# Sliding-window attention and SwiGLU on one core: transposes of k and q for chunks 0 to 9 in 64x64 tiles, and another order of the opening

## The chip, the core and the metric

The kernel runs on one NeuronCore of a Trainium2 chip. Five engines have a queue each: TensorE (PE; its weight loads are shown apart as PEld), VectorE (DVE), ScalarE (ACT), GpSimd (POOL) and SyncE (SP). They take their instructions in the order written and wait for one another by semaphores. DMA transfers are issued from the queues of POOL, SP and ACT. Matrix products go from SBUF into PSUM, which has eight banks; VectorE and ScalarE read PSUM. The metric is the device time of one execution in microseconds; less is better.

## What is computed

Attention with a causal window of 64 over 8 batches, 8 heads, 576 positions and head dimension 64, and then a SwiGLU block over the 4608 tokens (512 to 1536 to 512):

```python
scores = scale * np.matmul(q, k.transpose(0, 1, 3, 2))
mask = (rel >= 0) & (rel < window)            # rel = query position - key position, window = 64
scores = np.where(mask, scores, -1000000000.0)
attn = np.exp(scores - np.max(scores, axis=-1, keepdims=True))
attn = attn / (np.sum(attn, axis=-1, keepdims=True) + 1e-09)
x = np.matmul(attn, v)                        # heads side by side: 4608 x 512
g = x @ w_gate
out = (g * (1.0 / (1.0 + np.exp(-g))) * (x @ w_val)) @ w_out
```

Inputs and output are float32.

## The kernel before

The 4608 tokens are 36 chunks of 128 for the attention and 9 column blocks of 512 for the FFN; work for both is interleaved by hand in `build`, and the order of the calls there is the order on every engine. `_Graph.op` records each operation with the tiles it reads and writes; `emit` turns the data dependences into semaphore waits, one place in the queue of one engine for each operation. All matrix products of one operation are one unit: they wait together and signal together.

For a chunk n the attention is: transpose k and q so that the head dimension lies on partitions (`kT`, `qT`); scores into two PSUM banks (`Sb` or `Sk`; in the opening `Sa` with `Sbias`, which puts the mask in by a matmul, and `So`); exp on ScalarE into `pt`; attention times v with a column of ones (`AVs`, `AVmm`, `AVpair`); reciprocal and product on VectorE into `xb` (`AVn`, lines 623 and 626); transpose to `xT` (`Xp` on TensorE with an eviction, or an SP DMA transpose). `F(c, fs)` is a gate and value product of 4 + 4 matmuls (line 888), tanh on ScalarE (869), two VectorE products (874, 876). `O(c, u)` is 12 matmuls with Wo (930), an eviction and a store.

The transposes of k and q come in three kinds:

- Chunks 0 to 3, and 6 and 7: `first_T` (lines 825 and 827). For chunks 0 and 1 the float32 input is loaded by SP and ACT into two halves and cast by `first_cast` (lines 260 for ScalarE and 261 for VectorE); eight 128x128 transposes of k go into one bank, eight of q into another. For the other chunks the cast happens in the GpSimd DMA, and sixteen transposes with 128 input rows and 64 output rows fill one bank for two chunks. `first_ev` copies one chunk from the bank.
- Chunks 4, 5, 8 and 9: `T2` (line 382), sixteen such transposes for k and sixteen for q, a bank each, and one copy of 1024 columns for both chunks.
- From chunk 10 on: `T`, an SP DMA transpose. These the change leaves alone.

`bank` takes the least recently touched bank that isn't held, `pair` an even and the following odd one. In the opening the mask matmuls and the scores of chunks 0 to 3, the transposes, `AVs` and `Xp` take their banks by this rule. Copies of v by half a chunk (`shift`) give `AVs` its keys of the chunk before; two of the six are on VectorE (chunk 1), four on GpSimd.

Of the kernel before, what the change touches and what calls it, by code (L numbers as in the profile page):

```python
# [153 lines left out]
class _Kernel:  # L154
# [216 lines left out]
    def T2(self, st, x):  # L371
        src = (self.ks2 if x == "k" else self.qs2)[st % 2]
        dst = self.kT if x == "k" else self.qT
        nz = self.NZ if x == "k" else self.ZQ
        bank, bk = self.bank("a")
        tb = bank.bitcast(BF).rearrange("p (c j t) -> p c j t", c=4, j=2)

        def pe(e):
            for c in range(4):
                for j in range(2):  # L380
                    for p in range(2):
                        r = e.transpose(tb[64 * p:64 * p + 64, c, j, :], src[:, 2 * c + p, j, :], self.ident[:, :])  # L382
            return r

        self.g.op("pe", pe, reads=["ident", ("s2", x, st % 2, 0), ("s2", x, st % 2, 1)], writes=[bk])
        a = tb.rearrange("p c j t -> p c t j")

        def ev(eng, lo=0, hi=2):
            z0 = (2 * st + lo) % nz
            if z0 + hi - lo > nz:  # L390
                ev(eng, 0, 1)
                ev(eng, 1, 2)
                return
            d = dst[:, :, 128 * z0:128 * (z0 + hi - lo)].rearrange("p c (t j) -> p c t j", j=2)
            self.copy(eng, d, a[:, :, 64 * lo:64 * hi, :], [bk], [(x + "T", z, b) for z in range(z0, z0 + hi - lo) for b in range(2)])

        return ev

# [5 lines left out]
    def Sa(self, n, bias=False):  # L404
        st = [n, self.pair(), False]
        if bias:
            self.Sbias(st)
        return st
# [149 lines left out]
    def AVa(self, n):  # L558
        bx = self.pair()
# [215 lines left out]
    def Xp(self, n, kind="a"):  # L775
        ix, it, u = n % 4, (n // 4) % self.NX, n % 4
        xb, xo = self.xb[ix], self.xT[it][:, :, 128 * u:128 * u + 128]
        bank, bk = self.bank(kind)
# [37 lines left out]
    def first_T(self, x, st=0):  # L816
        c, ckeys = self.first[x, 1] if st else (self.first[x][2], self.first[x][3] + self.first[x, 0])
        bank, bk = self.bank("a")
        tb = bank.bitcast(BF).rearrange("p (j t) -> p j t", j=8)

        def pe(e):
            for j in range(8):
                if st:
                    for p in range(2):
                        r = e.transpose(tb[64 * p:64 * p + 64, j, :], c[:, j, p, :], self.ident[:, :])  # L825
                else:
                    r = e.transpose(tb[:, j, :], c[:, j, :, :], self.ident[:, :])
            return r

        self.g.op("pe", pe, reads=["ident"] + ckeys, writes=[bk])  # L830
        return bank, bk

    def first_ev(self, x, n, eng, b, after=None):
        bank, bk = b
        dst = self.kT if x == "k" else self.qT
        g = 16 * (n % 2)
        a = bank.bitcast(BF).rearrange("p (j g c) -> p c g j", j=8, c=4)[:, :, g:g + 16, :]
        d = dst[:, :, 128 * n:128 * n + 128].rearrange("p c (g j) -> p c g j", j=8)
        return self.copy(eng, d, a, [bk], [(x + "T", n, 0), (x + "T", n, 1)], after)
# [180 lines left out]
    def build(self):  # L1020
        F, S, AV, X, T2, O = self.F, self.S, self.AV, self.X, self.T2, self.O
# [36 lines left out]
        a2 = self.AVa(2)  # L1058
# [3 lines left out]
        x1 = self.Xp(1)  # L1062
        x1("act")
        a3 = self.AVa(3)
        self.AVs(a3)
        x2 = self.Xp(2)
# [19 lines left out]
        T2(2, "k")("act")  # L1086
        T2(2, "q")("act")
# [152 lines left out]
```

## Time and profile before

| | |
|---|---|
| runs | 326.6, 326.89, 327.25 us; median 326.89 |
| profiled execution | span 324.8 us; no other time of it is given, and against the median 2.09 us lie around the span |
| busy share of the span | PE 98%, DVE 66%, ACT 39%, POOL 32% |
| first FFN matmul (line 888) | starts at 15.63 us |
| DMA | 39.83 MB, mean 123 GB/s |
| largest groups on PE | line 888 111.2 + 111.0 us, line 930 98.8 us |

Times in the profile are microseconds from the start of the span. A timeline row gives the start, the length, the engine, the line, the operation, what it writes and reads, and how many instructions were merged into it; in brackets stands the idle time before it and what ended that. A row of the chain of waits gives start, length and the work that the end of the program goes back to. A row of a stretch gives, for each engine, the busy microseconds and the number of instructions; after them come the granted clock, the DMA share and GB/s. TensorE's instructions are pipelined, so that the start of the next one comes well before the end that is shown.

### The profile page before, as it was taken

The numbers are of one execution on the slowest core, as the hardware profiler recorded it, in microseconds if no ns is written. First come the engines' busy times: TensorE is split into PE (matmuls) and PEld (weight loads), VectorE is DVE, ScalarE is ACT, GpSimd is POOL, SyncE is SP. The second block draws the span as 40 slices with busy tenths as digits, with TensorE's granted clock in tenths as the row PEclk, the third lists the DMA queues.
The fourth block names the chain that finished last, engine by engine and source line by source line (L and its number), as shares of the span: only waits on it lengthen the run. The fifth ranks groups of instructions, "written<-read, shape, count | busy, mean of one in ns | idle before, by whom it ended". The sixth has DMA issues, their size and how long they took to land.

```text
span 324.8 us, 7717 instructions
## 1 busy us (share of the span) xinstructions
PE 319.2 (98%) x3278; PEld 162.4 (50%) x3278; DVE 215.8 (66%) x400; ACT 125.8 (39%) x224; POOL 104.2 (32%) x134
## 2 busy tenths in 40 slices
PE   6999999999999999999999999999999999999996
PEld 5665565564544454545454444545454544444444
DVE  5886866688485966676768585958576767555510
ACT  3935563634332443333333242424242422222311
POOL 6999831142626061607060607060402000000000
DMA  7999999999999899959998998999687202000012
GB/s 189 179 191 186 205 172 167 161 150 149 158 138 167 128 100 137 163 109 152 119 115 122 146 141 81 146 132 163 71 110 96 69 32 67 32 34 32 32 67 97
DMA packets 154354, 39.83 MB, mean 123 GB/s; under 512 B 140368, under 2 KB 149328, under 8 KB 154320
## 3 DMA queue, kind: packets, MB, share of 16 engines
q0 software_dynamic: 104896, 18.36, 72.8%
q1 hardware_dynamic: 43952, 11.15, 24.7%
q10 hardware_dynamic: 5472, 9.83, 9.5%
q8 instruction: 26, 0.43, 0.5%
q14 instruction: 8, 0.07, 0.1%
HBM read 37.75 MB, written 9.44 MB: 145 GB/s over the span
## 4 chain that ended last, share of the span: by engine, by line
PE 96%; DMA 1%; ACT 1%; DVE 0%; SPq 0%; issue 0%
PE ps L888 58%; PE ps L930 29%; PE ps L692 2%; PE ps L514 2%; DMA hT<-in_q_dram 1%; PE ps L464 1%; PE ps L825 1%; ACT pt L447 1%; PE ps L382 1%; PE ps L420 1%; PE ps L582 1%; PE ps L468 0%; DVE ost L261 0%; PE ps L784 0%; PE ps L439 0%; ACT xT L260 0%
## 5 line engine op out<-in xcount | busy, mean ns | idle before, releaser
L874 DVE SCALAR_TENSOR_TENSOR uu<-sig,ps 128x512 bf16<-128x512 bf16 x108 | 73.9, 685 | 57.3 <-ACT sig L869 57.1
L888 PE MATMUL ps<-xT,Wg 128*128 128x512 bf16 (+1 forms) x456 | 111.2, 369 | 0.1
L888 PE MATMUL ps<-xT,Wv 128*128 128x512 bf16 (+1 forms) x456 | 111.0, 368 | 0.0
L869 ACT ACTIVATE sig<-ps 128x512 bf16<-128x512 f32 x108 | 65.1, 603 | 89.0 <-PE ps L888 89.0
L930 PE MATMUL ps<-Wo,hT 128*128 128x512 bf16 (+1 forms) x444 | 98.8, 374 | 0.0
L876 DVE SCALAR_TENSOR_TENSOR hT<-uu,ps 128x512 bf16<-128x512 bf16 x108 | 74.2, 687 | 3.7
L888 PEld LDWEIGHTS ps<-xT,Wv 128*128 128x128 bf16 x456 | 44.5, 98 | 48.4
L930 PEld LDWEIGHTS ps<-Wo,hT 128*128 128x128 bf16 x444 | 43.3, 98 | 49.2
L888 PEld LDWEIGHTS ps<-xT,Wg 128*128 128x128 bf16 x456 | 42.7, 98 | 45.5 <-ACT xT L260 0.6
L330 POOL DMA_DIRECT2D kn<-in_k_dram x29 | 24.9, 861 | 107.7 <-PE ps L888 103.7
L330 POOL DMA_DIRECT2D va<-in_v_dram x40 | 34.4, 889 | 34.0 <-PE ps L888 34.0
L260 ACT ACTIVATE ost<-ps 128x512 f32<-128x512 f32 (+1 forms) x22 | 12.9, 587 | 52.9 <-PE ps L930 52.9
L261 DVE COPY ost<-ps 128x512 f32<-128x512 f32 (+1 forms) x15 | 10.1, 674 | 30.1 <-PE ps L930 30.1
L524 ACT ACTIVATE pt<-ps 128x512 bf16<-128x512 f32 x36 | 18.6, 603 | 29.0 <-PE ps L514 29.0
L330 POOL DMA_DIRECT2D qn<-in_q_dram x29 | 25.1, 870 | 0.3 <-issue 0.3
L476 ACT ACTIVATE pt<-ps 128x512 bf16<-128x512 f32 x28 | 14.5, 603 | 12.9 <-PE ps L468 12.9
L727 DVE TENSOR_TENSOR xb<-ps,rc 128x512 bf16<-128x512 f32 (+2 forms) x39 | 18.8, 510 | 0.5
L692 PE MATMUL ps<-va,pt 64*64 64x65 bf16 x800 | 12.3, 192 | 0.0
L490 DVE TENSOR_TENSOR pt<-pt,kmask 128x1024 bf16<-128x1024 bf16 x18 | 11.5, 683 | 0.0
L692 PEld LDWEIGHTS ps<-va,pt 64*64 64x64 bf16 x800 | 10.3, 107 | 0.0
L723 DVE RECIPROCAL rc<-ps 128x8 f32<-128x8 f32 (+2 forms) x39 | 5.7, 174 | 6.5 <-PE ps L692 6.5
L490 DVE TENSOR_TENSOR pt<-pt,mask 128x1024 bf16<-128x1024 bf16 x14 | 9.3, 686 | 0.9 <-ACT pt L476 0.8
(76 smaller groups left out, 131.6 us busy)
## 6 DMA issues: line engine op xcount, KB each, us to landing
out_dram<-ost ACTq DMA_DIRECT2D x35, 256.0 KB, 2.9
va<-in_v_dram POOLq DMA_DIRECT2D x32, 128.0 KB, 5.5
kn<-in_k_dram POOLq DMA_DIRECT2D x23, 128.0 KB, 4.2
qn<-in_q_dram POOLq DMA_DIRECT2D x23, 128.0 KB, 4.5
Wg<-in_moe_w_gate_dram POOLq DMA_DIRECT2D x6, 256.0 KB, 6.6
Wv<-in_moe_w_val_dram POOLq DMA_DIRECT2D x6, 256.0 KB, 7.4
Wo<-in_moe_w_out_dram POOLq DMA_DIRECT2D x2, 768.0 KB, 15.3
ks<-in_k_dram POOLq DMA_DIRECT2D x2, 256.0 KB, 7.1
```

The source lines that it names most:

```text
L260: return self.g.op("act", lambda e: e.activation(d, a, ACTF.Copy), reads=reads, writes=writes, after=after)
L330: self.g.op("pool", lambda e, d=d, a=a: e.dma_start(d, a), writes=ks, dma=True, after=gate)
L476: g.op("act", lambda e, po=po, p=p: e.activation(po, sv[p], ACTF.Exp, scale=SCALE), reads=[bx[p][1]], writes=[pk[p]])
L490: self.g.op("dve", lambda e: e.tensor_tensor(pt, pt, m, ALU.mult), reads=pk + mk, writes=pk)
L524: g.op("act", lambda e, po=po, p=p: e.activation(po, sv[p], ACTF.Exp, scale=SCALE), reads=[bx[p][1]], writes=[pk[p]])
L692: x = e.matmul(o, ab[0], ab[1], start=first, stop=phase == 1, skip_group_check=True)
L727: g.op("dve", lambda e, av=av, hs=hs, w=w, rc=rc, xo=xo: e.tensor_tensor(xo[:, :, hs, :], av[:, :, :, 0:64], rc[:, :, hs].unsqueeze(3).to_ ...
L869: g.op("act", lambda e: e.activation(sig[:, 0:w], G[:, 0:w], ACTF.Tanh, scale=0.5), reads=[gk], writes=[("sig", i)])
L874: g.op("dve", lambda e: e.scalar_tensor_tensor(uu[:, 0:w], sig[:, 0:w], 1.0, G[:, 0:w], ALU.add, ALU.mult), reads=[("sig", i), gk], writes ...
L876: g.op("dve", lambda e: e.scalar_tensor_tensor(out, v3(uu), 0.5, v3(V), ALU.mult, ALU.mult), reads=[("uu", i), vk], writes=[("hT", ih, f) ...
L888: r = e.matmul(bank[:, a * n:a * n + n], W[:, kk, f * 128:f * 128 + 128], xT[:, kk, lo:hi], start=(kk == 0), stop=(kk == NK - 1))
L930: r = e.matmul(OB[:, 0:n], hT[:, f, 128 * u:128 * u + 128], self.Wo[:, f, lo:hi], start=(f == 0), stop=(f == NF - 1))
```

## The change

All transposes of chunks 0 to 9 on TensorE become 64x64: source rows 0 to 63 and 64 to 127 are transposed apart, with the matching quarter of the identity, and each row half goes to a bank of its own. With the order in which k and q are loaded, a row half is a chunk, so there is a bank per chunk. `T2` and the use of `first_T` for chunks 6 and 7 give way to `T64`, which does k and q of two chunks in one operation of 64 transposes (k in the first half of a bank, q in the second) and hands out four evictions of 512 columns; `Tkq2` puts all four on ScalarE. `first_T` for chunks 0 to 3 does 32 transposes into a pair of banks and hands out two evictions.

In the opening the pairs of banks are given by hand (`at`). ScalarE casts all of the second half of q, of which VectorE did five eighths; of the evictions of chunks 0 to 3, ScalarE has q0, k1 and q2 where it had q0, q2 and q3. The mask matmul of chunk 0 comes ahead of q's transposes, scores 0 and 1 come ahead of the second batch of transposes, `AVs(0)` ahead of scores 2 and 3, and VectorE's second shift behind the first `AVn`.

```diff
-    def pair(self):
+    def pair(self, at=None):
...
-        ok = [j for j in range(0, 8, 2) if not {j, j + 1} & self.held]
+        ok = [j for j in range(0, 8, 2) if not {j, j + 1} & self.held and at in (None, j)]
...
-    def T2(self, st, x):
...
+    def T64(self, st):
+        n = 2 * st
+        bx = self.two()
+        loads = []
+        for x in "kq":
+            if st == 3:
+                loads.append((x, *self.first[x, 1]))
+            else:
+                loads.append((x, (self.ks2 if x == "k" else self.qs2)[st % 2], [("s2", x, st % 2, i) for i in range(2)]))
...
+            for i, (x, src, _) in enumerate(loads):
+                for a in range(8):
+                    for u in range(2):
+                        r = slice(64 * u, 64 * u + 64)
+                        for p in range(2):
+                            o = bx[u][0].bitcast(BF)[64 * p:64 * p + 64, 512 * i + 64 * a:512 * i + 64 * a + 64]
+                            y = src[r, a, p, :] if st == 3 else src[r, 2 * (a // 2) + p, a % 2, :]
+                            z = e.transpose(o, y, self.ident[r, r])
+            return z
+
+        rd = ["ident"] + [k for _, _, ks in loads for k in ks]
+        self.g.op("pe", pe, reads=rd, writes=[b[1] for b in bx])
+
+        def ev(x, u, eng):
+            bank, bk = bx[u]
+            i = "kq".index(x)
+            a = bank.bitcast(BF)[:, 512 * i:512 * i + 512]
...
+            self.copy(eng, d, a, [bk], [(x + "T", z, 0), (x + "T", z, 1)])
+            left.discard((x, u))
+            if not any(v == u for _, v in left):
+                self.held.discard(bk[1])
+
+        left = {(x, u) for x in "kq" for u in range(2)}
         return ev
+
+    def Tkq2(self, st):
+        ev = self.T64(st)
+        for u in range(2):
+            for x in "kq":
+                ev(x, u, "act")
...
-    def first_T(self, x, st=0):
+    def first_T(self, x, st, at):
...
-        bank, bk = self.bank("a")
...
+        bx = self.pair(at)
...
-                if st:
+                for u in range(2):
+                    r = slice(64 * u, 64 * u + 64)
                     for p in range(2):
-                        r = e.transpose(tb[64 * p:64 * p + 64, j, :], c[:, j, p, :], self.ident[:, :])
-                else:
-                    r = e.transpose(tb[:, j, :], c[:, j, :, :], self.ident[:, :])
...
+                        o = bx[u][0].bitcast(BF)[64 * p:64 * p + 64, 64 * j:64 * j + 64]
+                        z = e.transpose(o, c[r, j, p, :], self.ident[r, r])
...
     def build(self):
...
         self.first_cast("k", ((0, 0, 8, "dve"), (1, 0, 8, "act")))
-        self.first_cast("q", ((0, 0, 8, "dve"), (1, 0, 5, "dve"), (1, 5, 8, "act")))
-        fk = self.first_T("k")
-        self.first_ev("k", 0, "dve", fk)
-        fq = self.first_T("q")
-        q0 = self.first_ev("q", 0, "act", fq)
-        s0 = self.Sa(0, True)
-        self.first_ev("k", 1, "dve", fk)
-        self.first_ev("q", 1, "dve", fq, q0)
-        s1 = self.Sa(1, True)
+        self.first_cast("q", ((0, 0, 8, "dve"), (1, 0, 8, "act")))
+        fk = self.first_T("k", 0, 0)
+        s0 = self.Sa(0, True, 4)
+        fq = self.first_T("q", 0, 2)
+        fk(0, "dve")
+        fq(0, "act")
+        fq(1, "dve")
+        fk(1, "act")
+        s1 = self.Sa(1, True, 6)
         self.So(s0)
-        fk = self.first_T("k", 1)
-        self.first_ev("k", 2, "dve", fk)
         self.So(s1)
-        self.first_ev("k", 3, "dve", fk)
-        s2 = self.Sa(2, True)
-        fq = self.first_T("q", 1)
-        self.first_ev("q", 2, "act", fq)
-        self.first_ev("q", 3, "act", fq)
+        fk = self.first_T("k", 1, 0)
+        fk(0, "dve")
+        fk(1, "dve")
+        fq = self.first_T("q", 1, 2)
+        fq(0, "act")
+        fq(1, "dve")
         self.early_loads()
-        s3 = self.Sa(3, True)
-        a0 = self.AVa(0)
+        s2 = self.Sa(2, True, 4)
+        a0 = self.AVa(0, 0)
         self.AVs(a0)
+        s3 = self.Sa(3, True, 6)
         self.So(s2)
+        self.So(s3)
         self.shift(1, 0, "dve")
+        self.AVn(a0)
         self.shift(1, 1, "dve")
-        self.AVn(a0)
-        a1 = self.AVa(1)
+        a1 = self.AVa(1, 2)
         self.AVs(a1)
-        self.So(s3)
-        x0 = self.Xp(0)
+        x0 = self.Xp(0, at=0)
...
-        T2(2, "k")("act")
-        T2(2, "q")("act")
+        self.Tkq2(2)
...
-        fk = self.first_T("k", 1)
-        self.held.add(fk[1][1])
-        fq = self.first_T("q", 1)
-        self.held.add(fq[1][1])
-        self.first_ev("k", 6, "act", fk)
-        self.first_ev("k", 7, "act", fk)
-        self.held.discard(fk[1][1])
+        ev = self.T64(3)
+        ev("k", 0, "act")
+        ev("q", 0, "act")
         X(4, "act")
         F(0, (11,), mid=lambda: X(5, "act"))
-        self.first_ev("q", 6, "act", fq)
-        self.first_ev("q", 7, "act", fq)
-        self.held.discard(fq[1][1])
+        ev("k", 1, "act")
+        ev("q", 1, "act")
...
-        T2(4, "k")("act")
-        T2(4, "q")("act")
+        self.Tkq2(4)
```

`AVa(2)`, `AVa(3)`, `Xp(1)` and `Xp(2)` get their banks by hand in the same way (4, 6, 1 and 2).

More of the change, by code (lines that the diff above doesn't have):

```diff
@@ L402, in var, with Sa @@
         return 1 if b0 else (2 if b1 else 0)
-    def Sa(self, n, bias=False):
-        st = [n, self.pair(), False]
+    def Sa(self, n, bias=False, at=None):
+        st = [n, self.pair(at), False]
         if bias:
@@ L773, in X, with Xp @@
         self.Xp(n, kind)(eng)
-    def Xp(self, n, kind="a"):
+    def Xp(self, n, kind="a", at=None):
         ix, it, u = n % 4, (n // 4) % self.NX, n % 4
         xb, xo = self.xb[ix], self.xT[it][:, :, 128 * u:128 * u + 128]
-        bank, bk = self.bank(kind)
+        bank, bk = self.bank(kind) if at is None else (self.ps[at], ("ps", at))
         self.held.add(bk[1])
@@ L814, in first_cast, with ev @@
             self.first[x, 0] = self.first.get((x, 0), []) + [("fc", x, e0, j0)]
-    def first_T(self, x, st=0):
+    def first_T(self, x, st, at):
         c, ckeys = self.first[x, 1] if st else (self.first[x][2], self.first[x][3] + self.first[x, 0])
-        bank, bk = self.bank("a")
-        tb = bank.bitcast(BF).rearrange("p (j t) -> p j t", j=8)
+        bx = self.pair(at)
         def pe(e):
             for j in range(8):
-                if st:
+                for u in range(2):
+                    r = slice(64 * u, 64 * u + 64)
                     for p in range(2):
-                        r = e.transpose(tb[64 * p:64 * p + 64, j, :], c[:, j, p, :], self.ident[:, :])
-                else:
[L827 to L839, printed above, removed]
+                        o = bx[u][0].bitcast(BF)[64 * p:64 * p + 64, 64 * j:64 * j + 64]
+                        z = e.transpose(o, c[r, j, p, :], self.ident[r, r])
+            return z
+        self.g.op("pe", pe, reads=["ident"] + ckeys, writes=[b[1] for b in bx])
+        def ev(u, eng):
+            n = 2 * st + u
+            bank, bk = bx[u]
+            a = bank.bitcast(BF)[:, 0:512].rearrange("p (j g c) -> p c g j", j=8, c=4)
+            d = (self.kT if x == "k" else self.qT)[:, :, 128 * n:128 * n + 128].rearrange("p c (g j) -> p c g j", j=8)
+            self.copy(eng, d, a, [bk], [(x + "T", n, 0), (x + "T", n, 1)])
+            self.held.discard(bk[1])
+        return ev
     def warm(self, count):
```

38 lines of the change are left out of this document (12 added, 26 removed).

## The prediction

> **What bounds the kernel now.** I read the page from the top, then the chain of waits, then the timeline of the stretches the change touches.
>
> ```profile
> span 324.8 us, 7717 instructions
> ...
> PE 319.2 (98%) x3278; PEld 162.4 (50%) x3278; DVE 215.8 (66%) x400; ACT 125.8 (39%) x224; POOL 104.2 (32%) x134
> ...
> PE   6999999999999999999999999999999999999996
> ```
>
> The reader is to see that TensorE is nearly full from the second slice on. The span is 324.8 us; the page gives no other time of this execution, and if it was a median run, 326.89 - 324.8 = 2.09 us lie around the span. I make the sum in the span and take it from 326.89.
>
> The second view is busy time by stretch; this row is the one from 10 to 15 us (PE, PEld, DVE, ACT, POOL, each with its count).
>
> ```profile
> 10.00:15.00 5.00, 4.71 (x132) 3.28 (x126) 4.66 (x10) 4.96 (x11) 4.44 (x8) 1.00 1.81 185
> ```
>
> ScalarE (4.96 of 5.00) and VectorE (4.66) are as full here as TensorE: the opening is a chain through three engines. From the third slice on TensorE has no hole. So two prices count: in the opening, when the first FFN matmul starts; behind it, every TensorE microsecond removed, as long as no wait takes its place. The chain of waits shows both.
>
> ```profile
> 6.39 1.04 DVE ost L261 x2
> ...
> 8.17 0.86 PE ps L420 x4
> ...
> 12.54 2.06 ACT pt L447 x4
> ...
> 15.63 1.05 PE ps L888 x8
> ...
> 28.16 1.01 PE ps L382 x32
> 29.17 1.83 PE ps L888 x8
> ...
> 37.83 1.01 PE ps L825 x32
> ...
> 45.35 2.59 PE ps L930 x12
> ...
> 55.46 1.01 PE ps L382 x32
> ```
>
> The three transposing stages behind the opening (28.16, 37.83, 55.46) cost 1.01 us each, wholly on the path.
>
> **The stages 2, 3 and 4.** Each is 32 transposes of 128x64 now and becomes 64 of 64x64, in four quarters of the array, rows 0-63 writing one bank and rows 64-127 the other. No transpose of this form is in the trace. The nearest row is AV2's first half, the same tile, 64 or 65 columns moving, the same order of quarters, one bank per row half (columns of the first fence: PE, PEld).
>
> ```profile
> 35.12:35.39 0.27, 0.27 (x32) 0.27 (x32) 1.00 1.14 190
> ...
> 28.09 0.64 PE L382 MATMUL ps<-ident,ks 128*64 128x128 bf16 x16
> 28.56 0.61 PE L382 MATMUL ps<-ident,qs 128*64 128x128 bf16 x16
> 28.77 1.02 ACT L260 ACTIVATE kT<-ps 128x1024 bf16<-128x1024 bf16 x1 [0.84 <-PE ps L382]
> 29.11 1.04 PE L888 MATMUL ps<-xT,Wg 128*128 128x512 bf16 x4
> 31.43 2.06 ACT L476 ACTIVATE pt<-ps 128x512 bf16<-128x512 f32 x4 [0.23 <-PE ps L468]
> 31.57 1.04 PE L888 MATMUL ps<-xT,Wg 128*128 128x512 bf16 x4
> ```
>
> 32 start in 0.27 us, so 64 take 0.54. The 16 old ones take 28.56 - 28.09 = 0.47, and 29.11 - 28.56 = 0.55 with the change of tile behind them, so that change is 0.08. New stage: 0.54 + 0.08 = 0.62 against 1.02, 0.40 us less. Bounds: 0.45 less if the step is a shade quicker, and on the other side no overlap of the quarters at all (the first rival).
>
> The evictions go from two of 1024 columns to four of 512 on ScalarE, all behind the whole batch. Stage 2, from the batch's start: last tile starts at 0.54 and ends about 0.2 later, ScalarE starts at 0.77; four copies like the four exps (2.06) end at 2.83. TensorE does F(0,7) meanwhile (1.83 in the chain), so it is at S2(4) at 0.62 + 1.83 = 2.45. Chunk 4 has its k and q by then (first two copies); chunk 5's scores come half of the S2 stretch later (31.57 less 28.09 + 1.02 + 1.83 = 30.94 is 0.63, half is 0.31), at 2.76, and wait for the fourth copy until about 2.89. So 0.12 of the 0.40 turns into a new wait: 0.28 net. Queued behind are F(0,8) on TensorE, the tanh of F(0,7) and the exps on ScalarE; these start about 0.2 later in the stage, but no later in time. Stage 4 has the same neighbours: 0.28.
>
> Stage 3 has X(4) and X(5) in its place.
>
> ```profile
> 38.78 0.40 PE L784 MATMUL ps<-ident,xb 128*128 128x128 bf16 x4
> 39.88 0.39 PE L784 MATMUL ps<-ident,xb 128*128 128x128 bf16 x4
> 40.30 0.60 ACT L260 ACTIVATE xT<-ps 128x512 bf16<-128x512 bf16 x1 [0.28 <-PE ps L784]
> 40.96 1.04 PE L888 MATMUL ps<-xT,Wg 128*128 128x256 bf16 x8
> ...
> 25.89 0.71 POOL L808 DMA_DIRECT2D qs<-in_q_dram  x1
> ...
> DMA to landing us min/median/max: 10.1/10.5/11.0
> ```
>
> TensorE would be at F(1,(0,1)) 0.62 + 40.96 - 38.78 = 2.80 after the batch's start. ScalarE does two copies (from 0.77, 0.49 apart, which is 2.06 less one run of 0.6, by three), X(4)'s at 1.75, X(5)'s at 2.24, ending at 2.84: 0.09 of wait, 0.31 net. The batch now needs k and q at once; q lands at 25.89 + 11.0 = 36.89. The stage starts at 37.76 now, and 0.15 + 0.28 earlier it is at 37.33: nothing waits, with 0.4 to spare.
>
> The first O group (45.35 in the chain) reads all of Wo, a transfer that no engine speeds up, and caps what can be won ahead of it:
>
> ```profile
> L350 POOL DMA_DIRECT2D Wo<-in_moe_w_out_dram x2: 826/836/845, 26.6 to 27.4; - x2
> ...
> DMA to landing us min/median/max: 13.8/15.3/16.7
> ```
>
> It lands at 27.4 + 16.7 = 44.1; the cap is about 1.1 us, and I take 0.74 ahead of it. The bank order behind the opening I followed by the least-recently-touched rule: pairs 4/5 and 6/7 change places, and each group takes a bank from the same predecessor as before. I cost that at nothing. The loads that stand at another line (early_loads) keep their place in GpSimd's queue, between the same neighbours, and SP's queue isn't touched.
>
> **The opening.** The same work in another order; each instruction has a row.
>
> ```profile
> 4.78 0.63 ACT L260 ACTIVATE ost<-hT 128x512 bf16<-128x512 f32 x1 [1.14 <-DMA hT<-in_k_dram]
> 5.52 1.01 PE L827 MATMUL ps<-ident,ost 128*128 128x128 bf16 x8
> 6.22 0.36 ACT L260 ACTIVATE ost<-hT 128x192 bf16<-128x192 f32 x1 [0.80 <-DMA hT<-in_q_dram]
> 7.56 0.61 PE L827 MATMUL ps<-ident,ost 128*128 128x128 bf16 x8 [1.03 <-DVE ost L261]
> 8.96 0.40 PE L439 MATMUL ps<-qT,kT 64*128 64x128 bf16 x8
> 9.40 2.06 ACT L447 ACTIVATE pt<-ps 128x512 bf16<-128x512 f32 x4 [0.60 <-PE ps L439]
> 9.97 1.29 DVE L261 COPY kT<-ps 128x512 bf16<-128x512 bf16 x2 [0.44 <-PE ps L825]
> 11.27 0.87 DVE L261 COPY vs<-va 64x512 bf16<-64x512 bf16 x2
> 11.41 1.08 ACT L260 ACTIVATE qT<-ps 128x512 bf16<-128x512 bf16 x2
> 11.75 0.41 PE L607 MATMUL ps<-va,pt 128*128 128x65 bf16 x8
> 12.44 0.69 DVE L626 TENSOR_TENSOR xb<-ps,rc 128x512 bf16<-128x512 f32 x1
> 12.52 1.93 POOL L261 COPY vs<-va 64x512 bf16<-64x512 bf16 x3
> ```
>
> Casts: VectorE does one q half instead of one and 5/8, so it ends near 7.0, not 7.42; ScalarE's becomes 0.63, to 6.85. Score bias 0 now runs between k's and q's transposes, and at this point eight transposes still take 1.01 us against 0.61 later, so I take bias 0 (half of 0.86) at double and q's batch from 7.1 instead of 7.56. Its 32 small ones take 0.27 + 0.2, to 7.55. ScalarE copies q0 and then k1 (two: 1.08) to 8.7; VectorE k0 and q1. Scores 0 start at 8.25 (before 8.96), their exps once ScalarE is free, 8.66 to 10.72 (before 9.40 to 11.46): 0.74 gained here.
>
> Then it is lost again. Scores 1 wait for k1 (8.75), the next k batch ends at 9.5, VectorE copies k2 and k3 to 10.84 and, new on it, q3 to 11.45 (ScalarE had it). AVs(0) is put into banks 0/1 and so waits for k3's copy, 10.9; bias 3 and scores 2 and 3 are queued behind it, 0.24 + 0.43 + 0.1 more, so scores 2 start at 11.65 and the next four exps run 12.1 to 14.15 (before 12.54 to 14.60): 0.45 left. VectorE after 11.4: shift 0.55, reciprocal and product 0.95, the second shift 0.3 to 0.6 (the two take 0.87 now), two more reciprocal and product pairs at 0.93: chunk 2's output is ready at 15.05 to 15.3. Its transpose X(2) stands ahead of the first FFN matmul, which starts 0.28 later: 15.35 to 15.6, against 15.63. So 0.03 to 0.28, and I take 0.15, the middle. If the slow rate of 5.52 lasts through q's batch, 0.24 more is late and the opening loses 0.1; if VectorE starts its copies 0.1 sooner, it gains 0.35.
>
> The second shift now meets GpSimd's three shift copies (12.52, 1.93). Before, the two VectorE shifts were done by 12.14, and took 0.87 for two. [...] No row here shows the two together.
>
> **Sum.** 0.15 + 0.28 + 0.31 + 0.28 = 1.02 us: 326.89 - 1.02 = 325.9. Bounds: 0.35 + 3 x 0.45 = 1.7 at best (325.2), a loss of 0.1 with stages that gain 0.1 each at worst of this case (326.7).
>
> **The rivals.** 0.2% is 0.65 us, about what a measurement of this kernel can tell from no change.
>
> First, slower: the four quarters don't run side by side when they transpose. One 65-column matmul alone is (0.41 - 0.19) / 7 = 0.031 us in the AVs row at 11.75; 64 of them are 2.0, 1.0 more than now, in three stages 3.0. The opening's four batches of 32 would take 1.0 against 0.5 to 0.6, two of them on its chain, about 0.9 more: 3.9 slower, 330.8. It decides from a stage of about 1.2 us on. Against it: 32 matmuls of this tile in 0.27 us, and the column pairs of transposes already overlapping (16 in 0.47, 0.03 each for 128 columns). I give it 0.07, and 0.04 that only the column pairs overlap: 32 x 0.031 = 1.0 per stage, no gain there, a later eviction by 0.4, 0.2 more wait each, together with the opening 327.3.
> [...]
>
> Second, the gain is there on TensorE but ScalarE takes it back: if four copies cost 0.6 each with their gaps, chunk 5's wait is 0.35 in stages 2 and 4 and 0.3 in stage 3, the stages give 0.05 to 0.1 each, and with an opening at nothing the time is 326.6. For it: ScalarE gets 0.2 us more per stage at a place where the next scores wait for it. Against it: 0.49 per copy in the row of four. 0.12.
>
> [...] 0.05. That the change does nothing at all isn't possible: the tiles are different.
>
> **Chances.** Forecast 0.72, nine in ten of it below 326.24. First rival 0.07 + 0.04, second 0.12, third 0.05. Faster 0.66; same 0.22 (nearly all of the second and third, half of the pairs case, most of the forecast's tail); slower 0.12 (the serial case, the other half of the pairs case, and 0.03 of the forecast for a wait on the way that I haven't seen). The range reaches from the best bound less a little for the runs, 325.1, to the pairs case, 327.3; it leaves out the serial case.
>
> **What would show it.** Right: each stage 0.6 to 0.65 us in the chain, 64 instructions of tile 64x64; a wait of TensorE on ScalarE's kT or qT of about 0.1 before the second scores of S2(4) and S2(8), and on xT before F(1,(0,1)); exps at 8.7 and 12.1; the first FFN matmul at 15.35 to 15.6 released by VectorE's xb. Wrong: stages at 1 us or more (first rival), a wait of 0.3 on ScalarE (second), a first FFN matmul after 15.7 (third), or a landing of q or Wo that ends TensorE's idle time.

## The result, and the profile after

The changed kernel is slower: 328.37 us (median of 8 runs, 327.46 to 331.22) against 326.54 for the kernel before beside it, a ratio of 1.0071 with a 95% interval of 1.0046 to 1.0096. The forecast was 325.9, and at most 327.3. The profiled execution took 329.31 us, with a span of 327.6; before, the span was 324.8. So 2.8 us have to be found in this execution. The three runs with a granted clock of 0.994 or 0.995, the profiled one among them, took 328.97 to 331.22 us and the five at 1.000 took 327.46 to 330.06, so by the clock the 3.41 us at half rate that are told of below were in those three alone (half of 3.41 is 0.005 of 327.6).

The first lines of the page after, and its row for the queue q8, of the kind "instruction" (transfers, MB, share of 16 DMA engines):

```profile
span 327.6 us, 8069 instructions
...
PE 319.0 (97%) x3454; PEld 161.6 (49%) x3454; DVE 215.2 (66%) x399; ACT 126.1 (39%) x227; POOL 104.1 (32%) x134
...
PE   7699999999999999999999999999999999999996
...
PEclk9989999999999999999999999999999999999999
...
q8 instruction: 27, 0.44, 0.6%
```

The same row of the page before:

```profile
q8 instruction: 26, 0.43, 0.5%
```

TensorE has 176 more matmuls (3454 less 3278) and as many more weight loads: 352 more instructions, in which nothing more is computed. The second slice of TensorE (8 to 16 us), 9 before, is a 6 now, and the granted clock has an 8 in the third. The timeline after, in the three places that matter (start, length, engine, line, operation, count, and in brackets the idle time ahead):

```profile
6.95 0.45 PE L846 MATMUL ps<-ident,ost 64*64 64x64 bf16 x32 [0.34 <-ACT ost L260]
...
8.55 2.06 ACT L467 ACTIVATE pt<-ps 128x512 bf16<-128x512 f32 x4
...
10.79 0.42 PE L627 MATMUL ps<-va,pt 128*128 128x65 bf16 x8
...
11.41 0.57 DVE L261 COPY vs<-va 64x512 bf16<-64x512 bf16 x1
11.57 0.64 PE L459 MATMUL ps<-qT,kT 64*128 64x64 bf16 x32
...
12.02 2.07 ACT L467 ACTIVATE pt<-ps 128x512 bf16<-128x512 f32 x4 [0.92 <-PE ps L459]
...
12.14 0.22 PE L627 MATMUL ps<-vs,pt 128*64 128x65 bf16 x1
...
12.29 0.19 PE L627 MATMUL ps<-vs,pt 128*64 128x65 bf16 x1
...
12.98 0.46 DVE L261 COPY vs<-va 64x512 bf16<-64x512 bf16 x1
14.36 0.19 PE L627 MATMUL ps<-vs,pt 128*64 128x65 bf16 x1 [1.88 <-issue]
...
14.45 0.19 PE L627 MATMUL ps<-va,pt 128*64 128x65 bf16 x1
...
17.20 1.73 PE L908 MATMUL ps<-xT,Wg 128*128 128x256 bf16 x8
...
30.33 0.45 PE L389 MATMUL ps<-ident,ks 64*64 64x64 bf16 x32
30.61 0.43 PE L389 MATMUL ps<-ident,qs 64*64 64x64 bf16 x32
30.97 1.04 PE L908 MATMUL ps<-xT,Wg 128*128 128x512 bf16 x4
...
32.99 0.22 PE L484 MATMUL ps<-qT,kT 64*64 64x128 bf16 x2
...
33.22 0.24 PE L484 MATMUL ps<-qT,kT 64*64 64x128 bf16 x2
...
39.80 0.45 PE L389 MATMUL ps<-ident,ks 64*64 64x64 bf16 x32
40.07 0.26 PE L389 MATMUL ps<-ident,qs 64*64 64x64 bf16 x10
41.30 0.38 PE L389 MATMUL ps<-ident,qs 64*64 64x64 bf16 x22 [0.97 <-issue]
41.60 0.40 PE L804 MATMUL ps<-ident,xb 128*128 128x128 bf16 x4
```

Up to 12.3 us this is nearly the opening that was forecast. Then TensorE stops in the middle of `AVs(1)`, after ten of its sixteen matmuls, which are one unit and whose operands are all there (the last of them, VectorE's first shift, ended at 11.98), and goes on 1.88 us later. In stage 3 it stops again, after ten of the 32 transposes of q: 0.97 us. "issue" as the releaser means that the profile shows nothing the engine waited for, and the weight load at the end of each hole has no semaphore to wait for. Stage 2, between the two, is as forecast.

The rows by stretch (PE, PEld, DVE, ACT, POOL, granted clock, DMA share, GB/s) show what follows the first hole:

```profile
14.00:16.00 2.00, 1.33 (x30) 1.06 (x29) 1.25 (x4) 0.68 (x2) 1.99 (x3) 0.80 1.44 195
16.00:18.00 2.00, 2.00 (x27) 1.54 (x26) 1.35 (x3) 1.16 (x2) 2.00 (x4) 0.50 1.45 197
```

The clock records of this trace have the rate at 0.5 from 15.19 us for 3.41 us. The first FFN matmuls, 8 of 256 columns, take 1.73 us where they took 1.05.

The sum, from starts of the same work in the two traces: the first FFN matmul at 17.20 instead of 15.63, +1.57; the next FFN groups at half rate, +2.2; stage 2 gives, and the matmul behind it is at 30.97 instead of 29.11, +1.86; after the wait in `S2(4)` +2.0; the transpose behind stage 3 at 41.60 instead of 38.78, +2.82; stage 4 gives, +2.5; its wait and the rest, +2.8 at the end. Both holes and the slow stretch are the whole loss of this execution; the stages give about what was said, and the loss is more than three times as large.

What the holes have in common is seen by counting TensorE's instructions (matmuls, weight loads and its sequencer's, in the order of the trace, from 0). The first hole is ahead of number 449, the second ahead of 1217, which is 449 + 3 x 256. The queue of the q8 row carries 16,384 bytes per transfer; in all thirteen traces it has as many transfers as there are such blocks in TensorE's stream from number 193 on (27 here, 26 before). One such transfer lies ahead of each hole; this is the DMA view of the stretch 11.9 to 12.9 us (queue and kind: transfers or packets, MB, share of an engine-time):

```profile
q0 software_dynamic: 504, 0.18, 154.1%
q8 instruction: 1, 0.02, 5.5%
```

It begins at 11.94, and TensorE goes on at 14.36, 2.42 us later. The one of the second hole begins at 38.80, and TensorE goes on at 41.30. In between, the loads of weights and inputs go on through the first queue. This gave the theory for the experiments, an estimate from these two holes, as no view shows a request. **Blocks:** TensorE's instructions come in blocks of 256; on entering one, the block after it is asked for; the transfer begins some microseconds later (3.2 and 4.3 at the two holes), among the loads; 2.4 to 2.5 us after it begins the block can run; and where 256 instructions take less than all this, TensorE stands still. Its rivals: **order** (some wait in the new order of the opening, or of stage 3's evictions, that the profile doesn't name) and **tiles** (64x64 transposes stall by themselves).

Before, the second block was entered at 11.81 us, the transfer began at 14.98, and instruction 449 was wanted at 18.38: 0.9 to 1.0 us to spare by the same 2.4. After, with 96 more instructions in the first two batches of transposes and 160 in the opening, the block is entered at 8.69 and 449 wanted at about 12.3.

### The profile page after: what moved, and what is told of

Read it like the earlier page. It is cut to its first block, busy times and chain, and to the rows that moved or that the text cites. A ratio compares the mean times of both kernels' runs of the same rounds, so it can differ in the third digit from the quotient of the medians.

```text
span 327.6 us, 8069 instructions
## 1 busy us (share of the span) xinstructions
PE 319.0 (97%) x3454; PEld 161.6 (49%) x3454; DVE 215.2 (66%) x399; ACT 126.1 (39%) x227; POOL 104.1 (32%) x134
## 4 chain that ended last, share of the span: by engine, by line
PE 95%; DMA 1%; issue 1%; DVE 1%; ACT 1%; ACTq 0%
PE ps L908 58%; PE ps L950 29%; PE ps L712 2%; PE ps L534 2%; DMA hT<-in_q_dram 1%; PE ps L484 1%; PE ps L804 1%; PE ps L389 1%; PE ps L602 0%; PE ps L627 0%; PE ps L488 0%; DVE kT L261 0%; PE ps L459 0%; PE ps L846 0%; PE ps L565 0%
## 5 line engine op out<-in xcount | busy, mean ns | idle before, releaser
L260 ACT ACTIVATE ost<-ps 128x512 f32<-128x512 f32 (+1 forms) x22 | 12.9, 588 | 52.9 <-PE ps L950 52.9
L712 PE MATMUL ps<-va,pt 64*64 64x65 bf16 x800 | 12.3, 192 | 0.0
## 6 DMA issues: line engine op xcount, KB each, us to landing
Wo<-in_moe_w_out_dram POOLq DMA_DIRECT2D x2, 768.0 KB, 15.4
```

The costliest lines, as they stand in the source:

```text
L260: return self.g.op("act", lambda e: e.activation(d, a, ACTF.Copy), reads=reads, writes=writes, after=after)
L712: x = e.matmul(o, ab[0], ab[1], start=first, stop=phase == 1, skip_group_check=True)
```

## The experiments

**The stages alone, and the opening alone.** Two kernels, each with one half of the change. The first has the build of before up to the FFN:

```diff
-        fk = self.first_T("k", 0, 0)
-        s0 = self.Sa(0, True, 4)
...
+        fk = self.first_T("k")
+        self.first_ev("k", 0, "dve", fk)
...
         self.Tkq2(2)
```

> The opening of before, the 64x64 stages 2, 3 and 4 of after. Theory A (TensorE runs out of instructions: the hole of 1.88 us in the opening and that of 0.96 us in stage 3 stand 768 = 3 x 256 TensorE instructions apart, and each ends 1.55 us after a 16 KB transfer of the instruction queue; the opening of after brings 160 more instructions in the same time): no hole in the opening, the first FFN matmul at 15.6 us, every stage 0.62 us, the hole of stage 3 gone from its place, and a hole of 0 to 0.8 us at some other instruction between 33 and 37 us; time 0 to 0.9 us under before. Theory B (the 64x64 transposes themselves hold TensorE up after some number of them, and the opening's hole is a wait for the shifted copies of v): a hole of about 1 us inside stage 3 again, time about that of before.

Measured: 328.57 us against 326.48 (ratio 1.0051, interval 1.002 to 1.0082). In the profiled execution of this kernel the first clock record, of full rate, is at 10.8 us only (in three of the ten traces with such records it is 10.8 to 13.4, in the others 4.95 to 7.6); ahead of it, from 8.23, four mask matmuls take 1.91 us, where they took 1.03 before, and the first FFN matmul is 1.38 us late; the quickest of its runs, 327.0 and 327.1, are some 0.6 above before. Timeline of stage 3, and of two places further on:

```profile
38.93 0.45 PE L389 MATMUL ps<-ident,ks 64*64 64x64 bf16 x32
39.21 0.43 PE L389 MATMUL ps<-ident,qs 64*64 64x64 bf16 x32
39.58 0.40 PE L804 MATMUL ps<-ident,xb 128*128 128x128 bf16 x4
...
59.72 0.22 PE L488 MATMUL ps<-qT,kT 64*64 64x64 bf16 x2 [0.37 <-issue]
...
66.13 0.44 PE L712 MATMUL ps<-va,pt 64*64 64x65 bf16 x26 [0.55 <-issue]
```

No hole in the opening and none in stage 3, which takes 39.58 - 38.93 = 0.65 us. But two new ones, at instructions 1729 and 1985 (193 + 6 x 256 and 193 + 7 x 256), in scores and attention products that the change doesn't touch. I had expected at most one, between 33 and 37 us, and no loss.

The second has the opening of the change and the stages of before:

```diff
-        self.Tkq2(2)
+        T2(2, "k")("act")
+        T2(2, "q")("act")
```

and so for stages 3 and 4.

> The opening of after, the stages 2, 3 and 4 of before (128x64 tiles, 1.01 us each). Theory A: a hole of 1.9 us in the opening at the same instruction (the ninth matmul of AVs(1)), none in stage 3; first FFN matmul near 17.2 us; 1.0 to 1.8 us over before. Theory B: the same hole too, as the shift stands in the same place.

Measured: 328.5 us, ratio 1.0076 (1.0047 to 1.0104). Timeline:

```profile
14.03 0.19 PE L655 MATMUL ps<-vs,pt 128*64 128x65 bf16 x1 [1.52 <-issue]
```

The same hole as in the change, at the same instruction 449, 1.52 us; none in stage 3; one of 0.88 us at instruction 1985, again in an attention product that is as before. No drop to half rate follows here, and the first FFN matmul is at 16.43 us, not near 17.2. So each half alone brings holes, and not only at its own instructions. That speaks against "tiles", not yet against "order".

**64 more instructions, and the loads later.** Two kernels, run once each. One has 38 matmuls of 16 columns on zeros in the warm-up in place of three of its five:

```diff
+            for _ in range(38):
+                r = e.matmul(bank[0:32, 0:16], self.wz[:, 0:32], self.wz[:, 0:16], start=True, stop=True)
...
-        self.warm(5)
+        self.warm(2)
```

> After, with 64 more TensorE instructions among the warm-up matmuls, where TensorE has nothing else to do (3 of the 5 warm-up matmuls go, 38 small ones come; the output doesn't depend on them). Theory A: the hole moves 64 instructions ahead, from the ninth matmul of AVs(1) to the scores of chunks 2 and 3, with about 1.1 us, and stage 3's hole leaves the place inside q's transposes. Theory B: both holes stay where they are.

Measured: 329.6 us. Both of the change's holes are gone, which I had not expected of the first; two others came, 1.31 us at instruction 1985 and 0.88 us at 2241. The first clock record, of full rate, is at 13.4 us here; ahead of it, at 5.17, the first 32 transposes take 0.64 us, where they took 0.45 in the change, and the first FFN matmul is at 16.8 us without a hole. So TensorE wanted instruction 449 later; that the refill was therefore in time is an estimate.

The other holds back the loads of six FFN weight blocks and the early loads until `AVs(3)`:

```diff
-        self.W(2, 4)
...
+        self.W(2, 4, a3[3][-1])
```

> After, with the weight loads for column blocks 2 to 7 and the loads of chunks 4 and 5 held back until AVs(3) is done, so that the DMA engines have little to do when the instruction transfer is due (the FFN waits for its weights later, so the total isn't to be compared). Theory A, with the time from the block's first instruction to the next block (5.7 us in the opening) set by the transfers ahead: the hole in the opening shrinks from 1.88 us to under 1. Theory A with a fixed time, or theory B: 1.9 us as before.

Measured: 335.3 us. The opening's hole shrank, but to 1.26 us and not under 1.0: the block's transfer began 2.8 us after the block before it was entered, where it was 3.2. Where the delayed loads then ran, the holes grew; the timeline of stage 3:

```profile
42.55 0.26 PE L389 MATMUL ps<-ident,qs 64*64 64x64 bf16 x10
45.67 0.37 PE L389 MATMUL ps<-ident,qs 64*64 64x64 bf16 x22 [2.87 <-issue]
```

It is the hole of the change, ahead of the same transpose, at 2.87 instead of 0.97 us. Its transfer began 6.3 us after the block ahead was entered, where it was 4.3. So the length isn't a property of the transposes; it moves with the transfers. Another hole, of 1.75 us, lies at instruction 961. This kernel moved other things too, and is no clean proof.

**Only the number of instructions.** The kernel before with no part of the change, but 108 more TensorE instructions in the warm-up, and its control, with 14 matmuls of 192 columns, 16 more instructions over the same time:

```diff
+            for _ in range(60):
+                r = e.matmul(bank[0:32, 0:44], self.wz[:, 0:32], self.wz[:, 0:44], start=True, stop=True)
...
-        self.warm(5)
+        self.warm(2)
```

> The kernel before with none of the change in it: every transpose, bank, cast and eviction as before. Only three of the five warm-up matmuls (12 TensorE instructions) give way to 60 small matmuls on zeros (120 instructions) that fill the same 2.4 us, so that everything behind them stands 108 instructions later in TensorE's instruction stream. Theory of instruction blocks (256 instructions each, two held, a refill takes 5 to 8 us while the loads run): the boundaries now fall where instructions are dense. From the entries and refills of the run before I work out holes of about 1.0 us near 14.1 us (ahead of or inside the second attention product) and about 2.1 us near 67 us, 3.1 us in all, some 329.5 us beside 326.5 for the kernel before; a hole lies at an instruction number that is 193 plus a multiple of 256 (449, 1985). Rival (the small tiles, or the order of the opening, make the holes): no tile and no order differs from before, so no hole and the time of the few-instruction control, within 0.3 us.

> The control of the run with 60 small matmuls: the same three warm-up matmuls give way to 14 longer ones on zeros that fill the same 2.4 us, so everything behind stands 16 instructions later (28 less 12). Theory of instruction blocks: from the entries and refills of the run before, no hole; 326.5 us plus or minus 0.3. If the warm-up's narrower matmuls let the clock come up later, the first FFN matmul is up to 1.1 us late, in this run and in the one with 60 alike. Rival: the same.

Measured: 326.67 us (ratio 1.0016, 1.0005 to 1.0027) and 326.49 (1.0003, 0.9986 to 1.002). The 3.1 us forecast for the first did not come. Its trace says why: the transfer for 449 began 2.5 us after the block ahead was entered and the one for 1985 0.7 us after, where I had reckoned with some 3 to 4 from the trace of before; TensorE was at these instructions at 13.78 and 65.88, that is 2.44 and 2.42 us after the transfers began, just as the blocks were in. The 2.4 us held; the time until a transfer begins is not a constant that can be carried from one kernel to another. This execution, 326.27 us, shows no stop over 0.2 us. Of the eleven runs five lie between 326.18 and 326.34 and six between 326.67 and 327.65, which is a little above before; whether the refill was late in these, no trace says. As a test of the theory this kernel is undecided.

**One stage at a time.** The control with 14 matmuls and stage 2's transposes of the change; and the kernel before with stage 3's, its warm-up 12 instructions shorter (two matmuls of 512 columns for five of 224):

```diff
-        T2(2, "k")("act")
-        T2(2, "q")("act")
+        self.Tkq2(2)
```

```diff
-        fk = self.first_T("k", 1)
...
+        ev = self.T64(3)
...
-        self.warm(5)
+        self.warm(2)
```

> The control with 14 matmuls, and of the change only the 64x64 transposes of stage 2 (chunks 4 and 5): 64 more TensorE instructions at 30 us. By the traces so far the stage gives 0.38 us and the wait of the second scores for the fourth eviction takes 0.17 back. Theory of instruction blocks: worked out from the entries and refills of before, all boundaries behind stage 2 move 64 instructions ahead and miss the dense places, no hole, so 0.2 us less than the control (326.3 beside 326.5), and after stage 4 the lead is still 0.2. Rival (the small tiles themselves bring holes): a hole of 0.5 to 1 us inside or right behind the stage's transposes, so 0.3 to 0.8 us more than the control.

> Of the change only the 64x64 transposes of stage 3 (chunks 6 and 7); before's opening, stages 2 and 4; the warm-up is 2 matmuls of 512 columns in place of 5 of 224, 12 instructions fewer. In the changed kernel the hole of 0.97 us lay inside just this stage. Theory of instruction blocks: with 12 instructions fewer ahead of it, the boundary at instruction 1217 falls behind the stage's transposes, no hole there; the stage gives 0.38 us, the wait behind it takes 0.07: 0.3 us less than before (326.2 beside 326.5), with at most 0.2 us of holes elsewhere. Rival (the tiles or the order of this stage's evictions make the hole): the hole of about 1 us stays in it, 0.6 us more than before.

Stage 2 alone: 326.32 us (ratio 1.0001, 0.9991 to 1.0011; the control 1.0003). Timeline:

```profile
27.22 0.45 PE L417 MATMUL ps<-ident,ks 64*64 64x64 bf16 x32
27.49 0.44 PE L417 MATMUL ps<-ident,qs 64*64 64x64 bf16 x32
27.86 1.04 PE L938 MATMUL ps<-xT,Wg 128*128 128x512 bf16 x4
```

The stage takes 0.64 us and there is no hole. Against the control's trace the work behind it gains 0.38 us and loses 0.17 to the wait in `S2(4)`; the 0.21 that is left stays until stage 4, as expected, but is too little for the runs to tell. So the tiles bring no hole by themselves.

Stage 3 alone: 326.56 us, ratio 1.002 (1.0002 to 1.0039), in two groups: seven runs from 326.01 to 326.61, five from 327.51 to 328.5. The profiled execution is one of the latter:

```profile
37.63 0.44 PE L417 MATMUL ps<-ident,ks 64*64 64x64 bf16 x32
40.12 0.45 PE L417 MATMUL ps<-ident,qs 64*64 64x64 bf16 x32 [2.04 <-issue]
40.49 0.40 PE L832 MATMUL ps<-ident,xb 128*128 128x128 bf16 x4
```

A hole of 2.04 us, but not where the change has it: ahead of the first transpose of q, not the eleventh. That is instruction 961 here, 193 + 3 x 256, a block's first again. I had looked to 1217, which is past the stage here, and taken 961's refill to be in time: the block ahead was entered at 30.93, its transfer began 6.8 us later, at 37.69, and TensorE went on 2.43 after that. That the refill is late in some executions only would explain the two groups, but only one of these was profiled. The quick group is the gain of 0.3 that was expected, as near as the runs can tell.

**The whole change, 16 instructions later.** If a hole belongs to a number, it must move in the program when the number does:

```diff
+            for _ in range(10):
+                r = e.matmul(bank[0:32, 0:88], self.wz[:, 0:32], self.wz[:, 0:88], start=True, stop=True)
...
-        self.warm(5)
+        self.warm(4)
```

> The changed kernel whole, with 16 more TensorE instructions in the warm-up: four warm-up matmuls and 10 small ones on zeros in place of five, over the same time. Theory of instruction blocks: a hole belongs to a number in the stream, so the hole of 1.88 us that stood ahead of the tenth matmul of the second attention product (instruction 449) now stands 8 matmuls earlier in the program, ahead of its second matmul or right at its start, 1.7 to 2.0 us long and ending 2.4 to 2.5 us after its block's transfer begins; the hole in stage 3 moves 8 transposes ahead too, or goes where its refill comes early. The time 328.4 plus or minus 0.8. Rival (something that the tenth matmul waits for): the hole stays ahead of the tenth.

Measured: 328.82 us, ratio 1.0067 (1.0046 to 1.0089). Timeline:

```profile
12.03 0.22 PE L627 MATMUL ps<-va,pt 128*64 128x65 bf16 x1
13.41 0.19 PE L627 MATMUL ps<-vs,pt 128*64 128x65 bf16 x1 [1.16 <-issue]
...
31.59 0.22 PE L484 MATMUL ps<-qT,kT 64*64 64x128 bf16 x2
33.98 0.25 PE L488 MATMUL ps<-qT,kT 64*64 64x64 bf16 x4 [2.17 <-issue]
```

The hole in `AVs(1)` now comes after two matmuls instead of ten: eight earlier, which are 16 instructions. By the weight loads it is eleven before the hole in the change and three here. The order, the tiles and the evictions are the same in both. In stage 3 the stop is still at 1217, and so has moved by 8 transposes too: q's third starts at 40.80, 0.17 us behind its second (in the change the eleventh was late), 2.23 us after the transfer began. And scores that ran without a stop in the change have one of 2.17 us, at instruction 961. Neither "order" nor "tiles" can move them so: both fall. The length of the first, 1.16, was under the 1.7 expected; its transfer began 2.8 us after the block's entry.

**The order without the small tiles.** The opening of the change with the 48 transposes of before, and the stages of before:

```diff
-        fk = self.first_T("k", 0, 0)
+        fk = self.old_T("k", 0, 0)
         s0 = self.Sa(0, True, 4)
-        fq = self.first_T("q", 0, 2)
+        fq = self.old_T("q", 0, 2)
```

> Of the change only the order of the opening, its shares of casts and evictions, and its banks for scores and products: the opening's transposes are those of before (48 in 128x128 and 64x128 tiles, 96 TensorE instructions, where the change has 128 in 256), one bank for both chunks, and stages 2 to 4 are as before. Theory of instruction blocks: the stream has the same count as before, the second block is entered near 11.5 us and 449 falls at the FFN's first matmuls, so no hole in the second attention product; the first FFN matmul at 15.4 to 15.9 us, 326.4 plus or minus 0.4 us beside 326.5. Rival (the order of the opening or its evictions hold TensorE up): the hole of 1.5 to 1.9 us between 12.5 and 14.4 us stays, 328.3 us.

Measured: 326.7 us, ratio 1.0006 (0.9993 to 1.002): no difference. Timeline:

```profile
11.48 0.42 PE L655 MATMUL ps<-va,pt 128*128 128x65 bf16 x8 [0.40 <-DVE kT L261]
...
13.82 0.40 PE L832 MATMUL ps<-ident,xb 128*128 128x128 bf16 x4 [0.52 <-DVE xb L674]
...
16.10 1.05 PE L961 MATMUL ps<-xT,Wg 128*128 128x256 bf16 x8
```

TensorE's waits have names here, kT and xb from VectorE, 0.40 and 0.52 us, and the hole of the change isn't there. The first FFN matmul is at 16.10 instead of the 15.4 to 15.9 expected; the order by itself brings nothing.

**What a refill takes when nothing else loads.** The kernel before, with 768 matmuls of 16 columns on zeros behind its last product:

```diff
         self.O_last(NFC - 1, 3)
+        self.tail(768)
```

> The kernel before, with 768 small matmuls (16 columns, on zeros) behind its last product: 1536 TensorE instructions, six blocks of 256, where no load runs any more. It measures what a refill takes by itself. Theory of instruction blocks: TensorE runs 128 matmuls at its own pace (20 ns each by the transposes, some 2.4 us) and then stands still until the next block is in, with about 0.9 us of transfer, 1.55 us behind it and some 0.5 us ahead of it, so holes of 0.3 to 1.0 us, each 128 matmuls behind the last; 15 us of matmuls and 2 to 5 us of holes, 343 to 348 us in all. Rival (refills are hidden when nothing else loads, or hold more than two blocks): no holes, 340 to 342 us.

Measured: 347.17 us. Timeline of the end:

```profile
323.74 16.27 PE L846 MATMUL ps<-wz 128*32 128x16 bf16 x611
340.43 4.67 PE L846 MATMUL ps<-wz 128*32 128x16 bf16 x157 [0.42 <-issue]
```

Two holes only, of 0.42 and 0.14 us, both at a block's first instruction (7873 and 8129, 256 apart), where I expected more. The matmuls took 25 to 27 ns each and not 20 (25.0 up to 328.46 us, 26.7 from there on, where the clock records have half rate), so that a block lasts 3.2 to 3.4 us, and the refill, begun 1.0 to 1.2 us after the entry, nearly keeps up; the two holes are where the transfer took 1.3 to 1.4 us instead of 0.95. So from entry to use a refill took, by estimate from the block's length and the holes, some 3.4 to 4 us with nothing else loading. While the loads run it is, with 2.42 us from the transfer's beginning on, 3.7 to 8.8 for the thirteen blocks that the kernel before and the change enter in the first 62 us, over 5 for twelve of them, and 9.2 (6.8 and 2.43) in the kernel with stage 3 alone.

The holes at a block's first instruction, from the traces' records of weight loads and instruction transfers (us):

| kernel | instruction | transfer begins | TensorE goes on | between |
|---|---|---|---|---|
| the change | 449 | 11.94 | 14.36 | 2.42 |
| the change | 1217 | 38.80 | 41.30 | 2.50 |
| stages alone | 1729 | 57.33 | 59.72 | 2.39 |
| stages alone | 1985 | 63.78 | 66.13 | 2.35 |
| opening alone | 449 | 11.35 | 14.03 | 2.68 |
| opening alone | 1985 | 63.55 | 66.15 | 2.60 |
| 64 more instructions | 1985 | 57.67 | 60.61 | 2.94 |
| 64 more instructions | 2241 | 64.96 | 67.32 | 2.36 |
| loads later | 449 | 11.18 | 13.48 | 2.30 |
| loads later | 961 | 34.49 | 36.95 | 2.46 |
| loads later | 1217 | 43.26 | 45.67 | 2.41 |
| stage 3 alone | 961 | 37.69 | 40.12 | 2.43 |
| 16 more instructions | 449 | 11.08 | 13.41 | 2.33 |
| 16 more instructions | 961 | 31.56 | 33.98 | 2.42 |
| 16 more instructions | 1217 | 38.57 | 40.80 | 2.23 |
| 768 at the end | 7873 | 337.46 | 340.43 | 2.97 |
| 768 at the end | 8129 | 341.52 | 344.15 | 2.63 |

Every one is at 193 plus a multiple of 256. Less the transfer's own time (0.88 to 1.55) the last column is 1.28 to 1.63 in all seventeen. Behind the warm-up no other weight load that has no semaphore to wait for is more than 0.3 us late in any of the thirteen traces.

## Why the prediction was wrong

**The stages: right.** 0.62 us was forecast; 30.97 - 30.33 = 0.64 in the change (0.68 in its stage 4), 0.64 and 0.65 in the kernels that have one stage or all of them without a hole there. The four quarters do overlap: 32 transposes start in 30.61 - 30.33 = 0.28 us, one every 8.8 ns, so the first rival, in both its forms, fell. The small matmuls of the last experiment, which all use one place of the array, took 25 to 27 ns each.

**The waits for the evictions: right in kind, a little small.** Forecast 0.12, 0.09 and 0.12, measured 0.16 (its place is between 32.99 and 33.22, the two chunks' scores in `S2(4)`), 0.07 and 0.15. The second rival fell with it: the gain isn't taken back there. Net of the waits a stage without a hole gives 0.2 to 0.3 us, some 0.7 for the three against the 0.87 forecast.

**The opening: right until it broke off.** Exps at 8.55 and 12.02 (forecast 8.66 and 12.1), `AVs(0)` at 10.79 (10.9), scores 2 at 11.57 (11.65). q's first batch began at 6.95 and not 7.1. Nor was VectorE late, to which the chances gave 0.05. The 0.15 in the forecast's sum is the middle of 0.03 to 0.28, and its lower end has 0.6 us for VectorE's second shift, which no run shows: in the change that shift ran 0.46 us from 12.98 with no idle time ahead of it, beside GpSimd's three copies, which took 1.93 us from 12.69, as long as before. Take the hole out of 17.20 and 15.32 is left, with the half rate from 15.19 on still in it, against 15.35 to 15.6. But the order's own worth, 0.15, isn't confirmed: with big tiles it is nothing.

**The step that failed** is the sum, and ahead of it "each instruction has a row" and the stages costed by the rate of the array. The change's 352 additional instructions were priced by how long TensorE takes to run them, which is less than before, and not by where they come from. The opening enters the block ahead of instruction 449 at 8.69 us, 3.1 us sooner than before, and is through it by 12.3; the transfer began at 11.94, and TensorE went on at 14.36. That is a hole of 1.88, one of 0.97 in stage 3 (which lost 0.79 by it where it should have gained 0.37), and, in the profiled execution, 0.7 to 0.8 for the stretch at half rate behind the first. The rows that could have said so were there: the page counts instructions for each engine and has a line for the instruction queue, and the trace of before has its second block, by the estimate above, 0.9 us ahead of need.

What the traces show of the blocks is a transfer of 16,384 bytes for every 256 of TensorE's instructions. The kernel before crosses from block to block without such a hole; this one lost 1.88 us at one crossing. No transfer began more than 42 instructions before TensorE was at the block ahead (39 in the trace of before, 40 in that of the change): the runs behave as if only the block that runs and the next were held.

The chances had 0.12 for slower and 0.03 of it for a wait not seen: too little for a change that adds 5% to the instructions of the busiest engine (352 to twice 3278).

What stays open: what starts a transfer, and how long it waits. At the holes it began 1.0 to 6.8 us after TensorE entered the block ahead, and without a hole also 0.7 and less (0.09 in the change, at 66.12); it was longer where loads were moved to (6.3 us instead of 4.3), but no run varies the loads alone. Among the FFN products further on it began up to 4.4 us before TensorE was at the block ahead (4.34 in the change, 4.28 before), so the request doesn't wait for TensorE to enter that block, as the theory has it. And the half rate: it follows the hole of 1.88 in the change and those of 1.26 and 2.87 in the kernel with later loads, and not that of 1.75 there nor those of 1.52, 1.31, 1.16 and 2.17 in others.

## What to carry to other kernels

Count an engine's instructions when a tile is cut smaller, not only its busy time: here the smaller tile gave TensorE its gain, 0.64 us a stage instead of 1.01, only where no block's first instruction came sooner than its refill, which by the estimates above took 3.4 to 4 us in a quiet place and mostly 5 to 9 while weights load. A hole with no releaser in the middle of one unit's matmuls was the sign; count to it, and see whether the next one lies a multiple of 256 away. Shifting the count by 16 or 64 instructions moved such holes, and as many or more were there afterwards; with the count of before the same opening had none, but no gain either. None of the kernels tried is measurably quicker than the one before.

## What the runs showed of the hardware

- At the 17 holes TensorE went on 1.3 to 1.6 us after the transfer ahead had ended, at 15 with loads running and at two without.
- The rate fell to 0.5 for 3.41 us three times, once in the changed kernel and twice in the one with later loads; in the changed kernel this began 10.24 us after its first record of full rate (4.95 to 15.19). Under the small matmuls behind the last product the rate fell at 328.46 and stayed at 0.5 to the end of the span at 345.3 (the record is 19.03 us long).
- What brings a drop is not shown: one followed the hole of 1.88 us, and none that of 2.17.
